# Six writes of x to DRAM, issued by ScalarE instead of SyncE

## The chip, the core and the metric

The kernel runs on one core of a Trainium2 chip. The time is that of one execution on the device in microseconds (us); the median of three runs before the change is 434.64 us (432.01 to 434.95). The trace is of one further execution of its own.

## What is computed

Three layers follow each other, all in float32: an attention with a decaying state (8 heads), a feed-forward layer with a short convolution as its gate, and a mixture of eight experts in which each token goes to one expert. The last two, cut to what matters here:

```python
def _moe_ref(x, w_in, conv_w, w_out):            # feed-forward with a gate
    h = np.maximum(x @ w_in, 0.0)
    ...
    gate = 1.0 / (1.0 + np.exp(-conv_out))       # conv over 3 neighbours in the sequence
    return (h * gate @ w_out)                    # the x of the next layer

def _moe2_ref(x, w_gate, w_local, w1, w2):       # one of 8 experts for each token
    ...
    for s in range(S):
        ...                                      # e: the token's expert, or the previous one's
        h = np.maximum(x[b, s] @ w1[e], 0.0)
        out[b, s] = p[e] * (h @ w2[e])
```

There are 2 batches of 768 tokens, 512 features, and 1024 hidden features in either layer.

## The kernel before

Attention and the feed-forward layer keep their data on the chip. The feed-forward output of a batch is made in six token tiles t = 0 to 5 of 128 tokens each (`ffn_out`): 24 matmuls add up a tile of 128 x 512 in PSUM (`x2_ps`, x_ps in the profile), ScalarE copies it to a tile in SBUF, and a DMA writes it to xs, a buffer in DRAM, whose rows are in the order of tokens. For t = 4 and 5 of the second batch (b = 1) the SBUF tile is one of two that stay (xl4, xl5, kept in `LAST`); for all others it is one of two buffers named xn, so that the third copy waits until the first write has landed.

While the second batch is in `ffn_out`, VectorE works out which expert each token has (`route`, then `tables`): ScalarE's two copies kp feed a scan on VectorE, a chain of small VectorE operations and four small groups of matmuls on TensorE follow, and at the end stand `ei` (the expert of each tile of tokens, read by SyncE to address weights) and `it` (the token numbers of each tile, read by GpSimd's gathers).

The expert stage then works on 11 tiles of 128 gathered tokens and two groups of four quarter tiles. GpSimd gathers a tile's rows from xs (`gather`, tile xg); the first two gathers read only rows of the tokens up to t = 3 of the second batch, and what belongs to t = 4 and 5 is added from xl4 and xl5 by matmuls (`begin_x`, `late_x`). Those first two start the stage on TensorE (L813). All later gathers read all of xs, so they wait for all six writes.

The weights of an expert are loaded by SyncE into a few buffers: `fetch(j, which)` issues four loads of 512 KB into a tile r, one for each (tile j modulo 2, which of the two matrices); `fetch_q` issues four such loads into a quarter buffer, qc or qs1l by turns. From the third tile on, a `fetch` carries a condition: where the same lane already holds that expert, its four loads are issued and move nothing. ScalarE and VectorE cut r into a high and a low part (`cut`, L717 and L718, tiles ws0h, ws0l, ws1h, wc), and TensorE multiplies with both.

The order on each engine is that of the code. SyncE therefore issues, in this order: the r loads of `fetch(0, 0)` and `fetch(0, 1)` (L698), the writes of t = 0, 1 and 2 of the second batch (L491), the loads of `fetch(1, 0)` (their address needs `ei`), the write of t = 3, four quarter loads qc (L708), the writes of t = 4 and 5, then `fetch(1, 1)`, four loads qs1l, and so on. A DMA issue waits on its engine's queue for its data, and everything behind it waits too. Each DMA also takes the next of eight counting semaphores by turns (DMAHW0 to DMAHW7 below) and waits until the DMA that had the same one eight DMAs earlier has landed.

Of the kernel before, what the change touches and what calls it, by code (L numbers as in the profile page):

```python
# [19 lines left out]
B, H, S, D = 2, 8, 768, 64  # L20
# [3 lines left out]
P = 128  # L24
# [67 lines left out]
def tile_kernel(ctx, tc, cat, cst, qT, kT, kN, vN, w_in, conv_w, w_out, wg, w1, w2, out):  # L92
    nc = tc.nc
    te, ve, se, po, sy = nc.tensor, nc.vector, nc.scalar, nc.gpsimd, nc.sync
# [11 lines left out]
    xs = dram.tile([NT, DM], F32, name="xs")  # L106
# [24 lines left out]
    def mm3(ps, lhi, llo, rhi, rlo, first, last):  # L131

        te.matmul(ps, lhi, rhi, start=first, stop=False)  # L133
        te.matmul(ps, lhi, rlo, start=False, stop=False)  # L134
        te.matmul(ps, llo, rhi, start=False, stop=last)  # L135
# [338 lines left out]
    def ffn_out(b, t, ms):  # L474

        ts = slice(t * P, (t + 1) * P)
        if ms[0] == 0:
            OUT[b, t] = psb.tile([P, DM], F32, tag="x2", name="x2_ps")
        ps = OUT[b, t]
        for m in ms:  # L480
            g = hg[b, m]
            mm3(ps, g[:, 0, ts], g[:, 1, ts], wo_hi[:, m, :], wo_lo[:, m, :], m == 0, m == 7)
        if ms[-1] == 7:
            if b == B - 1 and t >= NG - 2:
                xn = xpool[0].tile([P, DM], F32, name=f"xl{t}", bufs=1)
                LAST.append(xn)
            else:
                xn = rt.tile([P, DM], F32, name="xn", bufs=2)
            se.activation(out=xn, in_=OUT.pop((b, t)), func=AF.Copy)  # L489
            r = b * S + t * P  # L490
            sy.dma_start(out=xs[r:r + P, :], in_=xn)  # L491

    one_p = rt.tile([P, 12, P], F32R, name="one_p")
    mr = rt.tile([RK + E, S], F32R, name="mr")
# [248 lines left out]
    for t in range(2):  # L743
        ffn_out(0, t, range(6))
# [3 lines left out]
    for n, (t, ms) in enumerate(units, 1):  # L748
        ffn_out(0, t, ms)
        if n % 2 == 0 and n < 14:  # L750
            tick()
        if n in (3, 5, 7):
            next(side, done)
# [5 lines left out]
    for t in range(2):  # L759
        ffn_out(1, t, range(4))  # L760
# [302 lines left out]
```

## Time and profile before

| | before |
|---|---|
| median of three runs | 434.64 us (432.01 to 434.95) |
| the profiled execution | 432.95 us, of which the span of the trace is 431.2 us |
| TensorE (PE) busy | 408.8 us, 95% of the span |
| VectorE (DVE) busy | 289.6 us, 67% |
| ScalarE (ACT) busy | 259.2 us, 60% |
| GpSimd (POOL) busy | 91.5 us, 21% |
| moved by DMA | 86.59 MB, 201 GB/s over the span |
| granted clock of TensorE | 0.99 of full speed |

Times in rows count from the start of the span. In a timeline, each row has the start, the duration, the engine, the line of the program, the operation, the tile written and the tiles read, how many instructions are merged into the row, and in brackets how long the engine was idle before it and what released it. SPq is SyncE's queue of DMA issues. The feed-forward layer of the second batch ends at 244, and the expert stage fills the rest.

### The profile page before, as it was taken

To read this page: it belongs to the slowest core of one execution; us is meant where nothing else is said; L and a number is where in the kernel's file an instruction comes from. 1 tells how busy PE (TensorE), PEld (TensorE's weight loads), DVE (VectorE), ACT (ScalarE), POOL (GpSimd) and SP (SyncE) were. 2 spreads that over 40 slices of the span, in tenths; PEclk is the share of its full clock that TensorE was granted. 3 is DMA by queue.
4 is the path that set the end of the run, shared out by engine and by line. 5 is a ranking of instruction groups with operands and counts; after the bars stand their busy time and mean duration, and the time that the engine had idled before them with its cause. 6 is when DMAs were issued, how large, how long until landed. Compare 5 with 4: busy or idle time off the path is not lost.

```text
span 431.2 us, 7291 instructions
## 1 busy us (share of the span) xinstructions
PE 408.8 (95%) x2412; PEld 329.2 (76%) x2412; DVE 289.6 (67%) x518; ACT 259.2 (60%) x429; POOL 91.5 (21%) x92
## 2 busy tenths in 40 slices
PE   8898999999899999999999999999999999999991
PEld 7787897899798778988768776867738677776880
DVE  3798789787767260377899058968664796858650
ACT  2787677667666212566704166869556686958560
POOL 5256664211110000000000330305203132211210
PEclk9999999999899999999999999999999999999997
DMA  7989763230000101000197899999969999774100
GB/s 229 388 291 398 260 211 92 93 97 1 2 0 2 49 26 49 26 0 2 58 377 254 304 373 379 342 390 409 398 254 340 407 364 346 280 260 186 44 25 29
DMA packets 27324, 86.59 MB, mean 201 GB/s; under 512 B 3598, under 2 KB 4622, under 8 KB 27280
## 3 DMA queue, kind: packets, MB, share of 16 engines
q1 hardware_dynamic: 25200, 79.76, 50.4%
q0 software_dynamic: 2080, 6.29, 3.9%
q8 instruction: 21, 0.34, 0.3%
q14 instruction: 23, 0.19, 0.1%
HBM read 105.18 MB, written 6.55 MB: 259 GB/s over the span
## 4 chain that ended last, share of the span: by engine, by line
PE 35%; issue 26%; DMA 15%; DVE 14%; ACT 4%; POOL 3%; SPq 1%; POOLq 0%; DVEq 0%; ACTq 0%
DMA out_dram<-yo,it 13%; PE h_ps L133 5%; PE h_ps L134 4%; PE h_ps L135 4%; PE x_ps L133 4%; PE x_ps L134 3%; PE x_ps L135 3%; PE y L300 3%; DVE cc L353 3%; PE s_ps L282 2%; POOL xg L727 2%; PE inc L290 1%; DMA kq<-in_qT_dram 1%; PE y L302 1%; DVE na L149 1%
## 5 line engine op out<-in xcount | busy, mean ns | idle before, releaser
L133 PE MATMUL h_ps<-xT,wih 128*128 128x384 f32 x128 | 46.9, 366 | 0.0
L353 DVE SCALAR_TENSOR_TENSOR cc<-h,cw,cc 128x768 f32<-128x768 f32 x32 | 34.4, 1075 | 18.6 <-ACT cc L350 18.5
L863 POOL DMA_INDIRECT out_dram<-yo,it x13 | 16.7, 1282 | 136.3 <-ACT yo L862 136.3
L727 POOL DMA_INDIRECT xg<-xs,it x13 | 18.8, 1444 | 123.4 <-DMA qc<-in_w_dram 115.8
L134 PE MATMUL h_ps<-xT,wih 128*128 128x384 f32 x128 | 43.5, 340 | 0.0
L135 PE MATMUL h_ps<-xT,wil 128*128 128x384 f32 x128 | 43.4, 339 | 0.0
L133 PE MATMUL x_ps<-woh,hg 128*128 128x512 f32 x96 | 38.5, 401 | 0.0
L134 PE MATMUL x_ps<-wol,hg 128*128 128x512 f32 x96 | 37.6, 391 | 0.0
L135 PE MATMUL x_ps<-woh,hg 128*128 128x512 f32 x96 | 37.5, 391 | 0.0
L718 DVE TENSOR_TENSOR ws0l<-r,ws0l 128x1024 fp32r<-128x1024 f32 x22 | 26.0, 1221 | 16.3 <-ACT ws0l L717 16.2
L153 POOL TENSOR_TENSOR na<-na,raw 128x512 int32<-128x512 int32 (+1 forms) x17 | 21.9, 1289 | 48.9 <-ACT raw L151 17.7
L300 PE MATMUL y<-at,vz 128*128 128x128 f32 x192 | 30.6, 281 | 1.8 <-ACT vz L277 0.9
L718 DVE TENSOR_TENSOR ws0h<-r,ws0h 128x1024 fp32r<-128x1024 f32 x22 | 26.0, 1221 | 8.2 <-ACT ws0h L717 8.2
L718 DVE TENSOR_TENSOR wc<-r,wc 128x1024 fp32r<-128x1024 f32 x22 | 25.9, 1221 | 8.0 <-ACT wc L717 8.0
L717 ACT ACTIVATE ws0l<-r 128x1024 fp32r<-128x1024 f32 x22 | 22.1, 1052 | 13.9 <-PE y L135 13.9
L282 PE MATMUL s_ps<-qz,kq 128*128 128x256 f32 x96 | 29.2, 386 | 1.0 <-issue 1.0
L718 DVE TENSOR_TENSOR ws1h<-r,ws1h 128x1024 fp32r<-128x1024 f32 x22 | 26.0, 1221 | 6.0 <-ACT ws1h L717 3.8
L717 ACT ACTIVATE wc<-r 128x1024 fp32r<-128x1024 f32 x22 | 22.1, 1054 | 11.3 <-PE g L135 11.3
L300 PEld LDWEIGHTS y<-at,vz 128*128 128x128 f32 x192 | 25.4, 191 | 4.3 <-DVE xT L305 2.3
L284 DVE TENSOR_TENSOR at<-s_ps,ca 128x256 f32<-128x256 f32 x48 | 20.2, 420 | 11.7 <-PE s_ps L282 11.6
L133 PEld LDWEIGHTS h_ps<-xT,wih 128*128 128x128 f32 x128 | 24.6, 192 | 3.1 <-issue 1.8
L489 ACT ACTIVATE xn<-x_ps 128x512 f32<-128x512 f32 x10 | 6.0, 599 | 32.8 <-PE x_ps L135 18.2
(231 smaller groups left out, 1044.9 us busy)
## 6 DMA issues: line engine op xcount, KB each, us to landing
r<-in_w_dram SPq DMA_DIRECT2D x88, 512.0 KB
qc<-in_w_dram SPq DMA_DIRECT2D x32, 512.0 KB
qs1l<-in_w_dram SPq DMA_DIRECT2D x32, 512.0 KB
raw<-in_w_in_dram SPq DMA_DIRECT2D x8, 512.0 KB
raw<-in_w_out_dram SPq DMA_DIRECT2D x8, 512.0 KB
kq<-in_qT_dram SPq DMA_DIRECT2D x7, 384.0 KB
kq<-in_kT_dram SPq DMA_DIRECT2D x7, 384.0 KB
kv<-in_vN_dram SPq DMA_DIRECT2D x7, 384.0 KB
```

The lines of the kernel that those rows point to most:

```text
L133: te.matmul(ps, lhi, rhi, start=first, stop=False)
L134: te.matmul(ps, lhi, rlo, start=False, stop=False)
L135: te.matmul(ps, llo, rhi, start=False, stop=last)
L153: po.tensor_tensor(out=a, in0=a, in1=lo, op=ALU.add)
L282: te.matmul(ps, self.kq[:, 0, tok], self.qz[:, :, tok], start=True, stop=True)
L284: ve.tensor_tensor(out=self.at[c], in0=ps, in1=self.dm, op=ALU.mult)
L300: te.matmul(y, vz[:, c, j, :], at[:, j, :], start=(j == 0), stop=(c == 0 and j == 1))
L353: ve.scalar_tensor_tensor(out=cc, in0=h[:, i:i + S], scalar=cw[:, m, i:i + 1], in1=cc, op0=ALU.mult, op1=ALU.add)
L717: se.activation(out=w[:, 0, h, :], in_=r, func=AF.Copy)
L718: ve.tensor_tensor(out=w[:, 1, h, :], in0=r, in1=w[:, 0, h, :].bitcast(F32), op=ALU.subtract)
L727: return po.indirect_dma_start(out=xg, out_offset=None, in_=xs[0:n], in_offset=bass.IndirectOffsetOnAxis(ap=it[:, j:j + 1], axis=0), bound ...
L863: po.indirect_dma_start(out=out, out_offset=bass.IndirectOffsetOnAxis(ap=it[:, j:j + 1], axis=0), in_=yo, in_offset=None, bounds_check=NT ...
```

## The change

The write of x is issued by ScalarE (`se`) where the batch is the last one, and by SyncE (`sy`) elsewhere:

```diff
             se.activation(out=xn, in_=OUT.pop((b, t)), func=AF.Copy)
             r = b * S + t * P
-            sy.dma_start(out=xs[r:r + P, :], in_=xn)
+            (se if b == B - 1 else sy).dma_start(out=xs[r:r + P, :], in_=xn)
```

On ScalarE, from the softmax's exponential of the second batch (ex) onwards. xn is the tile copied from PSUM, kp the two copies that VectorE's scan reads:

```order
 L527 ACTIVATE ex<-d 128x48
 L489 ACTIVATE xn<-x_ps 128x512
+L491 DMA xs<-xn 128x512
 L535 ACTIVATE kp<-sp_2175 8x384
 L535 ACTIVATE kp<-sp_2176 8x384
-L489 ACTIVATE xn<-x_ps 128x512 x2
+L489 ACTIVATE xn<-x_ps 128x512
+L491 DMA xs<-xn 128x512
+L489 ACTIVATE xn<-x_ps 128x512
+L491 DMA xs<-xn 128x512
 L717 ACTIVATE ws0h<-r_2117 128x1024 x2
 L489 ACTIVATE xn<-x_ps 128x512
```

Each write stands right behind its copy; that of t = 0 now stands ahead of both kp.

On SyncE, between the quarter loads qc and the address of the loads r that follow them (TENSOR_LOAD ei reads an expert's number, ISA rows work out the address):

```order
 L708 ISA
 L708 DMA qc_2404<-in_w_dram 128x1024
-L491 DMA xs<-xl_2478 128x512
-L491 DMA xs<-xl_2506 128x512
 L679 TENSOR_LOAD ei
 L679 ISA x2
```

The two writes of t = 4 and 5 are gone from between the loads, and so are, further up, those of t = 0 to 3.

The first load of r behind them, in the program after the change, with what it waits for (semaphores of DMAs and of engines):

```order
L708 DMA qc_2404<-in_w_dram 128x1024 [waits DMAHW5_49]
L679 TENSOR_LOAD ei
L679 ISA x2
L698 ISA
L698 DMA r_2539<-in_w_dram 128x1024 [waits DMAHW6_49,PE_49]
```

The load now follows the qc loads directly and waits for TensorE, which reads what stood in the place of its buffer.

## Rows read from the trace of the kernel before

**Rows 1.** The page, busy time of TensorE in us, share, instructions

```profile
PE 408.8 (95%) x2412; PEld 329.2 (76%) x2412; DVE 289.6 (67%) x518; ACT 259.2 (60%) x429; POOL 91.5 (21%) x92
```

**Rows 2.** Timeline of SyncE's queue, 226 to 262

```profile
228.74 1.95 SPq L698 DMA_DIRECT2D r<-in_w_dram  x4
232.45 0.34 SPq L491 DMA_DIRECT2D xs<-xn  x1
233.58 4.00 SPq L708 DMA_DIRECT2D qc<-in_w_dram  x4
239.24 5.78 SPq L491 DMA_DIRECT2D xs<-xl  x2
245.85 2.97 SPq L698 DMA_DIRECT2D r<-in_w_dram  x4
```

**Rows 3.** Busy time in stretches; last two columns DMA's busy share, GB/s

```profile
224.00:230.00 6.00, 5.18 (x24) 3.95 (x23) 5.55 (x28) 2.50 (x3) 0.00 (x0) 1.00 0.55 204
...
244.40:247.50 3.10, 2.68 (x24) 2.71 (x25) 0.00 (x0) 0.27 (x1) 0.04 (x1) 1.00 0.47 120
...
262.00:310.00 48.00, 48.00 (x280) 33.90 (x273) 36.27 (x36) 35.89 (x47) 10.30 (x9) 1.00 0.99 385
...
319.00:324.00 5.00, 4.75 (x18) 1.35 (x19) 0.89 (x1) 0.67 (x1) 0.00 (x0) 1.00 0.20 56
```

**Rows 4.** Timeline of GpSimd, the first gather

```profile
239.27 1.21 POOL L727 DMA_INDIRECT xg<-xs,it  x1 [115.81 <-DMA qc<-in_w_dram]
```

**Rows 5.** Chain of work that ended last: start, us, what

```profile
244.69 2.00 DMA xs<-xl
...
247.47 1.00 POOL xg L727
```

**Rows 6.** Timeline of TensorE, its waits between 224 and 246

```profile
225.64 0.40 PE L621 MATMUL pb<-tb,cs 8*128 8x64 f32 x2 [0.82 <-DVE pi L558]
244.82 1.13 PE L813 MATMUL tp<-cs,xg 128*128 128x128 f32 x8 [0.79 <-DMA xg<-xs,it]
```

**Rows 7.** Timeline of ScalarE, 213 to 245

```profile
213.82 0.60 ACT L489 ACTIVATE xn<-x_ps 128x512 f32<-128x512 f32 x1 [0.45 <-PE x_ps L135]
214.68 0.85 ACT L535 ACTIVATE kp<-sp 8x384 f32<-8x384 f32 x2 [0.26 <-PE sp L532]
...
226.69 0.60 ACT L489 ACTIVATE xn<-x_ps 128x512 f32<-128x512 f32 x1 [8.07 <-DMA xs<-xn]
...
232.32 2.00 ACT L717 ACTIVATE ws0l<-r 128x1024 fp32r<-128x1024 f32 x2
...
244.07 0.60 ACT L489 ACTIVATE xl<-x_ps 128x512 f32<-128x512 f32 x1 [4.85 <-PE x_ps L135]
```

**Rows 8.** Timelines of TensorE and of SyncE's queue, 255 to 291

```profile
261.21 1.93 PE L892 MATMUL hq_ps<-qc,xq 128*32 128x512 f32 x16
...
263.19 3.69 SPq L708 DMA_DIRECT2D qc<-in_w_dram  x4
267.73 4.16 SPq L708 DMA_DIRECT2D qs1l<-in_w_dram  x4
...
286.54 3.68 SPq L708 DMA_DIRECT2D qs1l<-in_w_dram  x4
```

**Rows 9.** Timeline of TensorE, two quarter groups and what follows each

```profile
301.86 1.90 PE L914 MATMUL yq_ps<-qs1l,tq 128*32 128x512 f32 x16
303.69 0.50 PE L133 MATMUL y<-ws0l,th 128*128 128x512 f32 x1
...
317.90 3.24 PE L914 MATMUL yq_ps<-qs1l,tq 128*32 128x512 f32 x6
...
323.17 0.50 PE L133 MATMUL y<-ws0l,th 128*128 128x512 f32 x1
```

**Rows 10.** Chain of work that ended last, SyncE's first issues

```profile
1.19 0.42 SPq L234
1.66 0.42 SPq L236
```

**Rows 11.** Timeline of VectorE, the scan and the cut ws0l

```profile
215.19 0.94 DVE L540 TENSOR_TENSOR_SCAN mr<-kp,sp 8x384 fp32r<-8x384 f32 x1 [0.95 <-PE sp L532]
...
235.78 2.35 DVE L718 TENSOR_TENSOR ws0l<-r,ws0l 128x1024 fp32r<-128x1024 f32 x2
```

**Rows 12.** Line 698, 226 to 262: duration in ns, least, median, most

```profile
L698 SPq DMA_DIRECT2D r<-in_w_dram x16: 73/333/1357, 228.7 to 262.0; - x16
```

**Rows 13.** Tile xg, its gathers between 225 and 262

```profile
DMA to landing us min/median/max: 4.0/6.5/8.1
```

## The prediction

> **What bounds the kernel now.** I read the page first: TensorE is busy for 408.8 of 431.2 us [rows 1]. A TensorE that is busy for 95% of the span leaves little for a transfer to win, so the question is where TensorE stands still because of these six writes, directly or through what they delay. I therefore went from the writes outwards: the two queues that issue DMAs (SyncE and GpSimd), ScalarE, which makes the data, and TensorE, which waits for the gathers that read it.
>
> SyncE issues everything in program order. From 232.45 it carries, one behind the other, the write of token tile t = 3, four quarter-tile loads, the writes of t = 4 and 5, and then the loads r of the next stage [rows 2]. The row at 239.24 with 5.78 us holds both writes xl: SyncE issues that of t = 4 and then stands until ScalarE has copied t = 5, and only then can it go on to the r loads at 245.85. In those 5.8 us nothing new is loaded, and the DMA engines are 0.47 busy in 244.4 to 247.5 [rows 3]. That is the first thing the change can win.
>
> The second is on the way to TensorE. The first gather starts at 239.27 on GpSimd [rows 4]. It needs the writes of t = 0 to 3 in DRAM, and that of t = 3 was issued at 232.45: 6.8 us from issue to the reader's start. The row names a load of qc as releaser; that load is not among what the gather reads, the write ahead of it on the same queue is. On an empty queue a write takes 2.00 us from issue to landing, and the reader starts 0.78 us behind that (244.69 + 2.00 = 246.69; start at 247.47) [rows 5]. So some 4 us of the 6.8 are waiting behind loads. TensorE waits for this gather: 0.79 us of idle time ahead of 244.82 [rows 6].
>
> The third wait looks larger and is worth nothing: ScalarE stood idle for 8.07 us ahead of its copy of t = 2 at 226.69, released by the write of t = 0 (two buffers xn) [rows 7]. TensorE never waited for that copy: its wait in this stretch is 0.82 us at 225.64, and that is for VectorE's routing chain [rows 6].
>
> **The change, part by part.** *Six issues leave SyncE.* That chain of r loads no longer stands behind the copy of t = 5. What then holds it is its buffer, on top of tiles that TensorE reads in the matmuls of t = 5; so it goes out somewhere between 239.24 and 244.69, where it went out at 245.85: 1.2 to 6.6 us earlier. The qc loads at 233.58 no longer wait for the copy of t = 3; those of r at 228.74 can go when the expert numbers are read. DMA had a lull there too (0.55 busy in 224 to 230) [rows 3].
>
> *Where that lead goes.* I follow it along SyncE. The next load that needs something of TensorE is qc at 263.19: its buffer is read by the sixteen matmuls that start at 261.21 and last 1.93 us, to 263.14 [rows 8]. The load left 0.05 us later. However far SyncE has run ahead, it stands here until TensorE is through; from here it is ahead by what TensorE is ahead, no more. One thing may still be kept: the four qs1l issues at 267.73 took 4.16 us, the same four at 286.54 took 3.68 [rows 8]. I take the 0.48 us as one issue held by a full queue, and with fewer bytes outstanding I expect it to go.
>
> *What a lead is worth later.* There is one place in the expert stage where TensorE waits long for loads. The matmuls on qs1l of a quarter group take 303.69 - 301.86 = 1.83 us when their weights are there; those that start at 317.90 take 323.17 - 317.90 = 5.27 us [rows 9]. The loads are 3.44 us late. DMA is 0.99 busy in 262 to 310 and 0.20 in 319 to 324 [rows 3]. If the loads come earlier by G and 0.48 us and TensorE by G, the wait shrinks by 0.48 us.
>
> *Six issues come to ScalarE.* An issue at the start of SyncE's program takes 0.47 us from one to the next (1.19, 1.66) [rows 10]. Five of the six cost nothing: behind the copies of t = 1, 4 and 5 ScalarE idles, and the issue behind that of t = 3 pushes the cut ws0l, done at 232.32 + 2.00 = 234.32, to 234.8, where VectorE takes it up at 235.78 [rows 7, 11]; the cut behind t = 2 has more room still. If that cover were gone, each would cost its 0.47 us. The first is on the path. It stands between the copy of t = 0, which ends at 213.82 + 0.60 = 214.42, and the two copies kp that start at 214.68 [rows 7]; VectorE's scan waits for them at 215.19 [rows 11], and the routing chain from there is what TensorE waits for at 225.64. With 0.02 us to react and 0.47 us to issue, kp starts at 214.91: 0.23 us late, and TensorE is 0.23 us late from 225.64 on. If an issue on ScalarE costs as much as the longest load issue of the stage, 1.36 us [rows 12], it is 1.1 us. That is the upper bound; the lower one is nothing. I take 0.23, since a write's issue on SyncE is short (0.34 us at 232.45).
>
> *When the write of t = 3 lands.* Issued by ScalarE at about 232.5, it is no longer behind the r loads in one queue, but beside them. No row shows a write from ScalarE. Bounds: 2.00 us on an idle queue, and 2.00 + 4.1 = 6.1 where loads press, since the gathers, which have their own queue too, land after 4.0 to 8.1 us [rows 13], a spread of 4.1. That is 234.5 to 238.6, and the gather starts 0.78 later, at 235.3 to 239.4. I take the middle, 237.3. The gather itself then takes 4.0 to 8.1 us; with the 5.5 us that lie between 239.27 and the first matmul behind it at 244.82, that matmul could start at 242.8, before ScalarE's copy at 244.07 shows TensorE through with t = 5 [rows 7]. So the 0.79 us go.
>
> The Trainium skill ("DMA: Bandwidth & Descriptors", section "Queues, rings and completion order") says that SyncE and ScalarE each have a row of rings and that a DMA engine goes round between rows packet by packet. By it the write would be served in turn with the loads and would land, as an estimate, 0.6 us behind the idle-queue time; the spread of the gathers in rows 13 speaks for a slower share.
>
> *Sum.* TensorE ahead by 0.79 - 0.23 = 0.56 us, and 0.48 us of the later wait: 1.04 us. The profiled execution took 432.95 us (span 431.2), so 431.9 by its own count; it lies 1.7 us below the median of the runs shown, 434.64, which gives **433.6 us**. About 1% (4.3 us) is what a measurement here can tell from no change, and this is a quarter of it.
>
> **The rivals.** *The lead survives.* If qc at 263.19 is not held, or SyncE's lead is kept in DMA that is always full, the whole 3.44 us goes: 434.64 - 0.56 - 3.44 = 430.6. For it: DMA is 0.99 busy from 262 to 310 [rows 3], so what is ahead there has no gap to lose its lead in. Against it: the 0.05 us between TensorE's end and the issue.
>
> *Nothing moves.* The write lands as late as before because the loads take the engines anyway, 0.79 is not won, and only 0.23 is lost and at most 0.48 gained: 434.4 to 434.9. For it: the upper bound of the landing, 238.6, is where it was. The Trainium skill (same page, "Issuing engines are not separate DMA queues") would say this of the change: DMAs of all issuing engines share the engines and interleave, so that spreading them saves only the sequencer's time; the row at 239.24 shows that what is saved here is a wait on the sequencer, which such a rule does not price.
>
> *The other side: the gather comes later than now.* The qc and r loads now run ahead, DMA is full up to 244, and the write or the gather gets a small share. With both at their upper bounds the gather starts at 239.4 and lands at 247.5, 2.7 us behind 244.82: 434.64 + 0.23 + 2.7 - 0.48 = 437.1. If the write is served only once the loads have drained at about 244, it is some 439. It decides from a landing of the gather after 244.8; each microsecond beyond costs one. Against it: in rows 13 the second queue was always served beside full loads.
>
> *ScalarE's issue is dear.* At 1.36 us in front of kp, with 0.48 kept: 434.64 - 0.79 + 1.1 - 0.48 = 434.5, and with nothing won elsewhere 435.7.
>
> **How the numbers follow.** Main course 0.50; the lead survives 0.10; nothing moves 0.24; gather later 0.10; dear issue 0.06. The predicted time is the first's, 433.6. The range goes down to the second, 430.6, and up to the dear issue with nothing won and the lesser part of the late gather, 436.4; what is outside is the rest of the late gather and the runs' own spread (432.0 to 434.95). Over 1% faster (under 430.3) needs the surviving lead and a lucky run: 0.05. Over 1% slower (over 439) needs the late gather at its worst: 0.06. The rest is within 1%.
>
> **What the profile of the changed kernel would show.** SyncE's r loads leave before 245; if they do not, the wait on the buffer was the binding one. The first gather starts at 236 to 238, and the idle time ahead of the first matmul on xg is under 0.1 us. kp starts about 0.2 us behind its former place relative to the copy ahead of it. DMA is busy through 244 to 247. The qc issue still stands within 0.1 us of the end of the matmuls that free its buffer. The late quarter group takes about 4.8 us instead of 5.27. I am wrong in kind if that group takes 1.8 us (the lead was kept) or if the matmuls on xg start after 245.

## The result and the profile after

The changed kernel is slower: 438.53 us (median of 10 runs, 435.39 to 440.66) against 434.55 (432.01 to 435.81), a ratio of 1.0088 with a 95% interval of 1.0060 to 1.0117. Ratios, here and below, leave out executions in a disturbed state of the device, so they need not be the quotient of the medians. The difference is under the 1% that the prediction took as the least that can be told from no change; the interval is clear of 1 all the same. The prediction was 433.6, with a range up to 436.4. The profiled execution took 438.02 us, of which the span is 436.3.

The page, TensorE's busy time:

```profile
PE 411.0 (94%) x2412; PEld 332.1 (76%) x2412; DVE 289.5 (66%) x518; ACT 259.6 (60%) x429; POOL 92.4 (21%) x92
```

TensorE has the same 2412 matmuls as before [rows 1]. It is busy 2.2 us longer with them (411.0 against 408.8) and stands still 25.3 us of the span instead of 22.4. To find where, I measure from one event that both traces have, ScalarE's copy of token tile t = 5, to the first matmul g of the expert stage. That also takes out what differs ahead of it: the copy starts at 244.07 in the trace before [rows 7] and at 245.67 here, of which 0.15 us is the change (the copies of t = 0 and 5 lie 30.25 us apart before, 30.40 after) and the rest lies earlier and differs from execution to execution. First the kernel before (TensorE, then GpSimd's second gather):

```profile
246.68 1.06 PE L813 MATMUL tp<-cs,xg 128*128 128x128 f32 x8
...
250.21 0.50 PE L133 MATMUL g<-ws0h,xh 128*128 128x512 f32 x1
```

```profile
241.31 1.01 POOL L727 DMA_INDIRECT xg<-xs,it  x1 [0.28 <-POOL xg L726]
```

Then the kernel after (timelines of TensorE and of ScalarE; ACTq is ScalarE's queue of DMA issues):

```profile
227.25 0.40 PE L621 MATMUL pb<-tb,cs 8*128 8x64 f32 x2 [0.88 <-DVE pi L558]
248.23 2.05 PE L813 MATMUL tp<-cs,xg 128*128 128x128 f32 x8 [2.60 <-DMA xg<-xs,it]
250.07 1.71 PE L819 MATMUL tp<-oh,xl 128*128 128x128 f32 x8
252.01 1.13 PE L813 MATMUL tp<-cs,xg 128*128 128x128 f32 x8 [0.22 <-DMA xg<-xs,it]
252.98 2.84 PE L819 MATMUL tp<-oh,xl 128*128 128x128 f32 x24
255.61 0.49 PE L133 MATMUL g<-ws0h,xh 128*128 128x512 f32 x1
```

```profile
215.27 0.60 ACT L489 ACTIVATE xn<-x_ps 128x512 f32<-128x512 f32 x1 [0.45 <-PE x_ps L135]
215.90 0.35 ACTq L491 DMA_DIRECT2D xs<-xn  x1
216.29 0.85 ACT L535 ACTIVATE kp<-sp 8x384 f32<-8x384 f32 x2 [0.43 <-PE sp L532]
234.01 0.33 ACTq L491 DMA_DIRECT2D xs<-xn  x1
245.67 0.60 ACT L489 ACTIVATE xl<-x_ps 128x512 f32<-128x512 f32 x1 [4.85 <-PE x_ps L135]
```

From the copy of t = 5 to g: 6.14 us before (250.21 - 244.07), 9.94 after (255.61 - 245.67). That is +3.80 us, as much as the medians differ (3.98). From g to the end of the span nothing is lost: 180.99 before, 180.69 after. The 3.80 have two parts. Up to the first matmul on the gathered tile it is +1.81 (2.56 against 0.75: the wait for the first gather is 2.60 us instead of the 0.79 of [rows 6]). From there to g it is +1.99 (7.38 against 5.39): the first sixteen matmuls take 2.05 and 1.71 us, where [rows 6] has 1.13 for the first eight, and then the second gather is waited for (0.22 us). So it is the second gather that sets g here: its reader starts 6.34 us behind the copy, 2.61 before, and that +3.73 is nearly the whole. The matmuls that took longer ahead of it cost nothing in this trace, since the second gather lands at 251.9 (244.16 + 7.7) whatever they take.

The queues show why. GpSimd's gathers, SyncE's queue, and the stretches in the windows (DMA's busy share and GB/s are the last two columns, the column before them TensorE's granted clock):

```profile
242.12 1.21 POOL L727 DMA_INDIRECT xg<-xs,it  x1 [117.79 <-DMA qc<-in_w_dram]
244.16 1.01 POOL L727 DMA_INDIRECT xg<-xs,it  x1 [0.28 <-POOL xg L726]
```

```profile
232.29 3.73 SPq L708 DMA_DIRECT2D qc<-in_w_dram  x4
242.93 2.12 SPq L698 DMA_DIRECT2D r<-in_w_dram  x4
245.91 3.72 SPq L708 DMA_DIRECT2D qs1l<-in_w_dram  x4
```

```profile
244.40:247.50 3.10, 1.24 (x6) 0.68 (x4) 0.00 (x0) 0.60 (x1) 1.31 (x2) 1.00 0.93 326
247.00:250.00 3.00, 1.77 (x8) 1.80 (x9) 0.00 (x0) 0.00 (x0) 0.00 (x0) 0.67 1.03 384
250.00:253.00 3.00, 2.78 (x19) 2.62 (x18) 0.00 (x0) 0.00 (x0) 0.00 (x0) 0.76 1.03 413
```

Before, the r loads left 1.78 us behind the copy of t = 5 (245.85 [rows 2], 244.07). Now they leave 2.74 us ahead of it, at 242.93, between the two gathers. Before, DMA was 0.98 busy from 239.3 to 244.4. Then came the lull of [rows 3], 0.47 busy from 244.4 to 247.5, and at its start the two gathers landed (5.4 and 4.0 us behind their issue). It is 0.93 busy now: the loads are in it. The second gather is issued at 244.16 and its reader starts at 252.01; the two land 6.0 and 7.7 us behind their issue.

A second trace of the same kernel (439.12 us, span 437.3) shows the two parts larger:

```profile
247.87 1.13 PE L813 MATMUL tp<-cs,xg 128*128 128x128 f32 x8 [3.71 <-DMA xg<-xs,it]
248.83 1.49 PE L819 MATMUL tp<-oh,xl 128*128 128x128 f32 x8
250.98 2.05 PE L813 MATMUL tp<-cs,xg 128*128 128x128 f32 x8 [0.65 <-DMA xg<-xs,it]
252.82 4.42 PE L819 MATMUL tp<-oh,xl 128*128 128x128 f32 x24
257.03 0.50 PE L133 MATMUL g<-ws0h,xh 128*128 128x512 f32 x1
```

```profile
250.00:253.00 3.00, 2.35 (x11) 2.08 (x11) 0.00 (x0) 0.00 (x0) 0.53 (x1) 0.50 1.03 420
253.00:256.00 3.00, 3.00 (x16) 3.00 (x15) 0.00 (x0) 0.00 (x0) 2.57 (x4) 0.50 1.03 419
```

The copy of t = 5 starts at 244.19 here, so copy to g is 12.84 us, and from the copy to the end of the span it is 193.11 (187.13 before, 190.63 in the first trace). The last matmuls ahead of g run at half the clock (1.2 GHz, 0.50 in both rows): 2.05 and 4.42 us where the first trace has 1.13 and 2.84 for the same matmuls. That is 2.5 us in which no gather is waited for, so here the half clock is paid in full.

### The profile page after: what moved, and what is told of

Read it like the earlier page. It is cut to its first block, busy times and chain, and to the rows that moved or that the text cites. A ratio compares the mean times of both kernels' runs of the same rounds, so it can differ in the third digit from the quotient of the medians.

```text
span 436.3 us, 7289 instructions
## 1 busy us (share of the span) xinstructions
PE 411.0 (94%) x2412; PEld 332.1 (76%) x2412; DVE 289.5 (66%) x518; ACT 259.6 (60%) x429; POOL 92.4 (21%) x92
## 4 chain that ended last, share of the span: by engine, by line
PE 34%; issue 27%; DMA 16%; DVE 14%; ACT 4%; POOL 2%; SPq 1%; POOLq 0%; DVEq 0%; ACTq 0%
DMA out_dram<-yo,it 14%; PE h_ps L133 5%; PE h_ps L134 4%; PE h_ps L135 4%; PE x_ps L133 4%; PE x_ps L135 3%; PE x_ps L134 3%; PE y L300 3%; PE s_ps L282 2%; DVE cc L353 2%; DVE na L149 2%; DMA kq<-in_qT_dram 1%; PE inc L290 1%; DVE na L150 1%; PE y L302 1%
## 5 line engine op out<-in xcount | busy, mean ns | idle before, releaser
L300 PEld LDWEIGHTS y<-at,vz 128*128 128x128 f32 x192 | 25.3, 191 | 4.3 <-DVE xT L305 2.4
```

The lines of the kernel that those rows point to most:

```text
L300: te.matmul(y, vz[:, c, j, :], at[:, j, :], start=(j == 0), stop=(c == 0 and j == 1))
```

## The experiments

The theory was: SyncE's standing at its writes held the loads behind them back; without it they run ahead onto the two gathers that TensorE waits for. The first rival: writing from ScalarE is itself slow or costs time on the path. The last column is the stretch from the copy of t = 5 to g in the trace of one execution (two of the change, four of e8); each ratio is against the kernel before, run beside it. The traces of e2 and e4 are of short executions (431.53 and 431.82 us). Inserted lines shift the line numbers in some kernels by up to 6 (L816 and L819 are then the L813 of the kernel before).

| kernel | median, us (runs) | before, us | ratio, 95% interval | copy to g, us |
|---|---|---|---|---|
| before | | | | 6.14 |
| the change | 438.53 (10) | 434.55 | 1.0088 (1.0060 to 1.0117) | 9.94, 12.84 |
| e1_hold_all | 435.27 (12) | 434.25 | 1.0014 (0.9990 to 1.0038) | 6.06 |
| e2_hold_t5 | 434.24 (12) | 434.25 | 1.0000 (0.9975 to 1.0025) | 5.62 |
| e3_act_45 | 436.46 (12) | 434.25 | 1.0039 (1.0004 to 1.0074) | 9.47 |
| e4_act_03 | 433.76 (12) | 434.25 | 0.9990 (0.9965 to 1.0015) | 5.37 |
| e7_act_04 | 434.00 (12) | 434.42 | 1.0006 (0.9983 to 1.0029) | 5.42 |
| e8_r_first | 437.52 (6) | 434.42 | 1.0095 (1.0058 to 1.0132) | 7.58, 6.67, 11.94, 11.78 |
| e9_hold_half | 437.01 (6) | 434.42 | 1.0086 (1.0053 to 1.0119) | 7.86 |
| e5_r_behind_t3 | 436.19 (12) | 434.42 | 1.0045 (1.0017 to 1.0074) | 5.11 |
| e12_filler | 437.35 (6) | 433.87 | 1.0087 (1.0061 to 1.0113) | 10.27 |
| e15_filler3 | 436.78 (11) | 434.33 | 1.0066 (1.0030 to 1.0102) | 11.94 |

**Give SyncE its waits back (e1, e2).** Behind each write that ScalarE issues, SyncE issues a DMA of 256 bytes from the same tile to a spare buffer fz: in e2 for t = 5 alone, in e1 for all six (`range(6)` in place of `(5,)`).

```diff
             (se if b == B - 1 else sy).dma_start(out=xs[r:r + P, :], in_=xn)
+            if b == B - 1 and t in (5,):
+                sy.dma_start(out=fz[t:t + 1, :], in_=xn[0:1, 0:64])
```

> All six writes are issued by ScalarE, as in the change, and SyncE gets at each write's old place a DMA of 256 bytes that reads the same tile: it holds SyncE back as the write did and moves next to nothing. If the loss comes from SyncE running ahead with its loads (theory), the gathers come as early as before and the ratio is 0.998 to 1.002. If ScalarE's own way of writing is slow or its issues cost time on the path (rival), the holds change nothing: 1.004 to 1.009.

> As the change, with one such DMA of 256 bytes on SyncE at the place of the write of t = 5 only: the r loads behind it are held until ScalarE has copied t = 5, the qc loads are not. Theory: the two gathers have the quiet DMA again and land as fast as before, and what is left of the loss is the later start of the first gather, 1.25 us or up to 1.9 us: ratio 1.002 to 1.005. Rival (a slow way of writing or of issuing on ScalarE): no better than the change, 1.008.

e1 came out as the theory had it (1.0014). e2 did better than it: 1.0000, where 1.002 to 1.005 was expected. TensorE's first matmul on the gathered tile in e1, then in e2:

```profile
247.84 1.13 PE L816 MATMUL tp<-cs,xg 128*128 128x128 f32 x8 [0.71 <-DMA xg<-xs,it]
```

```profile
243.77 1.13 PE L816 MATMUL tp<-cs,xg 128*128 128x128 f32 x8
```

e1 has the wait of the kernel before (0.71 against 0.79 us), e2 has none. One wait of SyncE, that for the copy of t = 5, is all that separates e2 from the change, so it is the absence of this wait that brings the loss. The qc loads run ahead in e2 too, and that alone does no harm: the gather starts later (3.64 us ahead of the copy of t = 5, 4.80 before), but lands 3.5 us behind its issue, and the wait of 0.79 us is gone.

**Split the six writes (e3, e4, e7).** ScalarE issues only t = 4 and 5 in e3, t = 0 to 3 in e4 (`t < NG - 2`), t = 0 to 4 in e7 (`t < NG - 1`).

```diff
-            (se if b == B - 1 else sy).dma_start(out=xs[r:r + P, :], in_=xn)
+            (se if b == B - 1 and t >= NG - 2 else sy).dma_start(out=xs[r:r + P, :], in_=xn)
```

> Only the writes of t = 4 and 5 go to ScalarE; those of t = 0 to 3 stay on SyncE. The first two gathers read nothing that these two writes make. Theory: the r loads run ahead into the lull in which the two gathers landed, the gathers land later, and TensorE waits some 2 to 3 us more: ratio 1.004 to 1.007. Rival (slow writes on ScalarE): the gathers' own data come as before, 1.000 within 0.002.

> Only the writes of t = 0 to 3 go to ScalarE; those of t = 4 and 5 stay on SyncE and hold the r loads as before. Theory: the first gather starts up to 1.25 us later, since the qc loads run ahead of the write of t = 3, and the gathers themselves are as fast as before: ratio 1.001 to 1.004. Rival (slow writes or dear issues on ScalarE): these four carry the loss, 1.006 to 1.009.

> The writes of t = 0 to 4 go to ScalarE, that of t = 5 stays on SyncE, where it holds the r loads until ScalarE has copied t = 5. Theory (the r loads that run ahead of the copy of t = 5 are the whole loss, and the qc loads that run ahead are a small gain): ratio 0.997 to 1.001, and no idle time of TensorE ahead of its first matmul on xg. Rival (the six writes each carry a part of the loss): 1.005 to 1.008, five sixths of it.

In e3 the first two gathers read nothing that ScalarE writes, and TensorE waits for both; in e4 four of the six writes have moved, and nothing is late. e3, then e4 (TensorE, GpSimd's first gather and the lull):

```profile
248.87 1.13 PE L813 MATMUL tp<-cs,xg 128*128 128x128 f32 x8 [3.10 <-DMA xg<-xs,it]
...
251.67 1.13 PE L813 MATMUL tp<-cs,xg 128*128 128x128 f32 x8 [0.78 <-DMA xg<-xs,it]
```

```profile
239.61 1.21 POOL L727 DMA_INDIRECT xg<-xs,it  x1 [116.82 <-DMA qc<-in_w_dram]
```

```profile
243.36 1.13 PE L813 MATMUL tp<-cs,xg 128*128 128x128 f32 x8
```

```profile
244.00:247.00 3.00, 3.00 (x28) 2.94 (x27) 0.00 (x0) 0.11 (x1) 0.09 (x1) 1.00 0.61 175
```

e3 has both waits and 9.47 us from copy to g. Its median is below that of the change, with intervals that overlap, and its ratio is at the lower edge of what was expected; its trace ran at full clock. Part of the 9.47 us may not be the edit's: the first gather starts 3.58 us ahead of the copy of t = 5 instead of 4.80, on a path that e3 leaves alone (e8 below has executions of both kinds). In e4 the first gather takes at most 3.75 us from its issue to its reader (243.36 - 239.61), where before it was 5.55 (239.27 to 244.82), and TensorE waits for nothing. e4 expected a later gather and a loss of 0.4 to 1.7 us: the gather does start later, 3.90 us ahead of the copy of t = 5 instead of 4.80, and nothing is lost. e7 adds t = 4, and again nothing is lost. So five of the six writes can move without harm; the loss comes only when the sixth moves too.

**The loss without ScalarE (e8).** All writes stay on SyncE; `ffn_out` leaves the write of t = 5 in a list HELD5, and it is issued behind the r loads.

```diff
         fetch(1, 1)
+        HELD5.pop()()
         fetch_q(0, 0, 1)
```

> All writes stay on SyncE, as in the kernel before; only the order of its code changes: the write of t = 5 moves behind the four r loads that followed it, so that these leave some 2.9 us earlier, as they do after the change. ScalarE issues nothing. Theory: the loss is there without ScalarE, ratio 1.003 to 1.009, and TensorE waits 2 to 4 us ahead of its first matmul on xg. Rival (the loss belongs to the queue of ScalarE): 1.000 within 0.002.

> A second trace of the kernel with all writes on SyncE and the write of t = 5 behind the r loads. Its first trace was of its fastest execution (434.81 us, median 437.5) and shows only 0.5 us more between ScalarE's copy of t = 5 and the end of the span than before (187.63 against 187.13). Theory: an ordinary execution shows 189 to 191, with the loss ahead of the matmuls on xg. If it shows 187 to 188 again, the loss of the median lies ahead of the copy, and the theory does not explain this run.

> A third trace of the kernel with the write of t = 5 behind the r loads. Its two traced executions took 434.8 and 435.2 us and waited 2.0 and 1.1 us for the first two gathers at full clock; the four that were only timed took 435.6 to 439.8. If the rest of the loss is TensorE's clock, an execution of over 437 us shows a granted clock of 0.5 between 245 and 256 and one of under 436 shows 1.00.

> A fourth trace of the same kernel, for the same question: over 437 us with the granted clock at 0.5 between 245 and 256, under 436 us with 1.00.

1.0095: the loss is there with ScalarE issuing nothing. Its size differs between executions. The two that were traced first took 434.81 and 435.21 us, with waits of 0.4 to 1.3 us for each of the two gathers and the clock at 1.00. From the copy of t = 5 to the end of the span they have 187.63 and 188.19 us; e10 expected 189 to 191, and missed. This is the first:

```profile
246.02 1.13 PE L819 MATMUL tp<-cs,xg 128*128 128x128 f32 x8 [0.69 <-DMA xg<-xs,it]
...
249.35 1.13 PE L819 MATMUL tp<-cs,xg 128*128 128x128 f32 x8 [1.31 <-DMA xg<-xs,it]
```

The third and fourth took 440.50 and 439.30 us, with waits of 3.94 and 3.91 us and half the clock behind them, as expected of executions of over 437. The third:

```profile
249.30 2.05 PE L819 MATMUL tp<-cs,xg 128*128 128x128 f32 x8 [3.94 <-DMA xg<-xs,it]
```

```profile
250.00:253.00 3.00, 3.00 (x16) 3.00 (x15) 0.00 (x0) 0.00 (x0) 0.00 (x0) 0.50 1.03 407
```

From the copy to the end the third has 193.31 us, the fourth 192.34. The copy of t = 5 and the r loads come at the same time in the first and the third (copies at 245.37 and 245.39). The gathers do not. GpSimd's gathers and SyncE's r loads, in the first and then in the third:

```profile
240.46 1.21 POOL L733 DMA_INDIRECT xg<-xs,it  x1 [115.65 <-DMA qc<-in_w_dram]
242.63 1.92 SPq L704 DMA_DIRECT2D r<-in_w_dram  x4
```

```profile
242.31 1.21 POOL L733 DMA_INDIRECT xg<-xs,it  x1 [118.18 <-DMA qc<-in_w_dram]
242.65 1.93 SPq L704 DMA_DIRECT2D r<-in_w_dram  x4
244.34 1.01 POOL L733 DMA_INDIRECT xg<-xs,it  x1 [0.28 <-POOL xg L732]
```

In the first both gathers (the second at 242.50) start ahead of the loads; in the third the loads leave between the two, as in the change. All traces in which all four r loads leave ahead of the copy or all behind it, those with added matmuls and e5 left out, fall into four groups by this:

| r loads leave | first gather starts ahead of the copy of t = 5 by | copy to g, us |
|---|---|---|
| behind the copy (before, e1) | 4.7 to 4.8 us | 6.1 |
| behind the copy (e2, e4, e7) | 3.6 to 3.9 us | 5.4 to 5.6 |
| 2.7 us ahead of it (e8, first two) | 4.9 to 5.0 us | 6.7, 7.6 |
| 2.7 us ahead of it (the change, e3, e8's other two) | 3.1 to 3.6 us | 9.5 to 12.8 |

So a later gather alone costs nothing, the loads ahead of the copy with an early gather cost 0.5 to 1.4 us, and the two together 3.3 to 6.7. These are copy-to-g times of single executions, and within e8 the two kinds were seen, not made by an edit. In e8 the two kinds part well ahead of the gather: the copy of t = 2 waits 8.13 and 8.25 us for the write of t = 0 to land in the first two, 9.62 and 9.71 in the others, and the r loads of the first lane leave 1.4 to 1.5 us later behind it. Why that write lands later in some executions stays open.

**Half of the loads (e9).** As e2, with the DMA of 256 bytes between the second and the third of the four r loads.

```diff
         for i in range(4):
+            if (j, which, i) == (1, 1, 2):
+                sy.dma_start(out=fz[0:1, :], in_=LAST[1][0:1, 0:64])
             sy.dma_start(out=dst[:, i, :], in_=src[:, i * 1024:(i + 1) * 1024], **kw)
```

> As the change, with a DMA of 256 bytes on SyncE that reads the tile of t = 5, between the second and the third of the four r loads: two of them run ahead, two are held. If what counts is how many bytes of loads are under way beside the two gathers, the loss is about half of that with none held: 1 to 2.5 us, ratio 1.002 to 1.006. If any load ahead of the gathers makes them late by the full amount, 1.008; if two loads fit in the lull, 1.000.

```profile
246.88 1.13 PE L816 MATMUL tp<-cs,xg 128*128 128x128 f32 x8 [1.40 <-DMA xg<-xs,it]
...
249.78 1.13 PE L816 MATMUL tp<-cs,xg 128*128 128x128 f32 x8 [0.88 <-DMA xg<-xs,it]
```

The trace has about half of the loss (7.86 us, +1.72), the times have all of it (1.0086; the traced run, 436.06, is the shortest of the six). Whether the loss goes with the bytes stays open; that two loads of 512 KB are enough for a loss is shown.

**Let the gather start earlier (e5).** All writes on SyncE; the r loads of the first lane move behind the write of t = 3.

```diff
-        if n == 8:
+        if n == 12:
             fetch(1, 0)
```

> All writes on SyncE as before; the four r loads of the first lane (those that stood just ahead of the write of t = 3) are moved behind that write, so that it lands with little ahead of it. By the prediction's reading the first gather then starts some 3 to 4 us earlier and the 0.79 us of idle time of TensorE go: ratio 0.998. If the gather's own time under loads is what counts and not its start, the loads that now follow later lie on the gathers, and it is 1.000 to 1.004.

GpSimd's first gather, and the matmuls on a later gathered tile:

```profile
236.84 1.21 POOL L727 DMA_INDIRECT xg<-xs,it  x1 [112.65 <-DVE pr L665]
```

```profile
259.75 0.66 PE L800 MATMUL tp<-cs,xg 128*128 128x128 f32 x4 [3.37 <-DMA xg<-xs,it]
```

The gather no longer waits for a write (the row names VectorE, whose tables give the token numbers), and the wait of 0.79 us is gone, as the prediction's reading of an earlier gather had it. But the r loads now go out at 235.07 instead of 228.74, just ahead of the qc loads, and the writes of t = 4 and 5 land behind all eight. The third gather starts at 252.82 instead of 247.47, and TensorE waits 3.37 us for a later tile: 1.0045, the second of the two expectations and a little more. The trace is of one of the shorter of twelve executions (434.48 us) and has only 0.30 us more than before from the copy of t = 5 to the end of its span (187.43), so it does not show the whole of that loss.

**The half clock (e12, e15).** The change, with matmuls whose result nobody reads ahead of the first matmul on xg: six in e12, three in e15.

```diff
+        busy = psq.tile([P, 2, 512], F32, tag="q", name="busy")
+        for k in range(6):
+            te.matmul(busy[:, 0, :], ident, LAST[0], start=True, stop=True, skip_group_check=True)
         for j in range(2):
             begin_x(j)
```

> The changed kernel with six matmuls of TensorE added whose result nobody reads; they stand ahead of the first matmul on xg and need only xl4, so they run in the 2.6 to 3.7 us in which TensorE waits for the first gather. Both traces of the changed kernel show TensorE's granted clock at half (0.50) for 3.4 and 6.4 us right behind that wait. If the half clock adds to the loss (theory now): the clock stays at 1.00 there, the added matmuls are free, and the ratio falls from 1.0088 to 1.003 to 1.007. If the loss is the wait alone: 1.008 to 1.010, no better than the change.

> The changed kernel with three of the added matmuls instead of six. Six took 5.31 us, 2 us more than the wait, so that what they kept in clock they cost in time; three take 2.65 us and fit into the wait of 2.6 to 3.7 us. If the half clock adds to the loss: the granted clock stays at 1.00 from 244 to 256, the stretch from ScalarE's copy of t = 5 to the first matmul g takes 8 to 9 us (9.9 and 12.8 in the two traces of the change, 6.1 before), and the ratio is 1.004 to 1.007. If the wait alone counts: 1.008 to 1.010.

e12, then e15:

```profile
244.77 5.31 PE L940 MATMUL busy<-xl,cs 128*128 128x512 f32 x12
249.92 1.05 PE L813 MATMUL tp<-cs,xg 128*128 128x128 f32 x8
```

```profile
243.52 2.74 PE L940 MATMUL busy<-xl,cs 128*128 128x512 f32 x6
246.55 1.13 PE L813 MATMUL tp<-cs,xg 128*128 128x128 f32 x8 [0.30 <-DMA xg<-xs,it]
...
250.47 1.13 PE L813 MATMUL tp<-cs,xg 128*128 128x128 f32 x8 [1.89 <-DMA xg<-xs,it]
251.43 4.47 PE L819 MATMUL tp<-oh,xl 128*128 128x128 f32 x24
```

With six, the clock stays at full and the matmuls from 249.92 to g take 5.32 us, as before the change (5.39), but the six take 5.31 us, longer than either wait of the change (2.60 and 3.71), and the time is no better: 1.0087, on the side of "the wait alone". With three, the first wait is filled, but the second gather is waited for, and the clock halves behind that wait instead (4.47 us against 2.84); copy to g is 11.94 us where 8 to 9 was expected. 1.0066, with an interval that holds the full loss as well as a third of it. So neither run separates the two. The traces show that the half clock follows the waiting and adds to it in some executions (2.5 us in the second trace of the change, nothing in the first). How much of the median is its doing was not settled.

No version beat the kernel before by more than can be measured; e4, at 0.9990, is the nearest.

## Why the prediction was wrong

What happened is the rival "the gather comes later than now", priced at 437.1 to 439 and given 0.10, and the sign that the prediction gave for being wrong in kind: the matmuls on xg start after 245, at 248.23. That the price holds the measured 438.53 is in part luck: it has the first gather 2.7 us late, which is 1.81 us late in the first trace, and neither the second gather nor the clock. By the prediction's own steps:

- **The six issues on ScalarE: right.** An issue takes 0.33 to 0.35 us, and kp starts 1.02 us behind the copy's start instead of 0.86, 0.16 us later (0.23 predicted). TensorE's wait at pb is 0.88 (0.82 before).
- **The wait of 8.07 us ahead of the copy of t = 2: worth nothing, right.** It is gone, and the matmuls behind come no earlier.
- **The r loads leave earlier: right.** They leave 4.5 us earlier against the copy of t = 5, inside the 1.2 to 6.6.
- **The lead is lost at the next qc load: right.** The matmuls that free its buffer, and the load on SyncE's queue:

```profile
266.62 1.92 PE L892 MATMUL hq_ps<-qc,xq 128*32 128x512 f32 x16
```

```profile
268.61 3.70 SPq L708 DMA_DIRECT2D qc<-in_w_dram  x4
```

  It leaves 0.07 us behind their end (268.54). So the loads that ran ahead onto the gathers bought nothing later, and the rival in which the lead survives is out.
- **The late quarter group, 4.8 us: wrong, by little.** From 323.31 to the matmul that follows it at 328.48 it takes 5.17 us, 5.27 before; 0.10 of the 0.48 us.

```profile
323.31 1.25 PE L914 MATMUL yq_ps<-qs1l,tq 128*32 128x512 f32 x4
...
328.48 0.50 PE L133 MATMUL y<-ws0l,th 128*128 128x512 f32 x1
```

- **The write of t = 3: too small a term.** I took the middle of two bounds, a gather that starts 4.8 us behind the issue. It starts 8.1 us behind it (234.01 to 242.12), beyond my upper bound of 6.9. The lower bound, 2.00 us "on an empty queue", was not read on an idle one either: it is from the lull, where DMA was 0.47 busy. The Trainium skill ("DMA: Bandwidth & Descriptors", section "Queues, rings and completion order") has the two queues served in turn, by which I worked out a landing of 2.6 us as an estimate, a gather some 3.4 us behind the issue; the 8.1 us do not show that. This term also left out that the qc loads now leave ahead of this write (232.29, 234.01) and no longer behind it. In e1, where they wait again, ScalarE's write is 6.99 us ahead of its gather (235.51, 242.50), as SyncE's was (6.82). By itself this error costs nothing: in e4 the gather starts 7.8 us behind the issue (231.84, 239.61), and TensorE does not wait. But it puts the r loads between the two gathers, and e8 shows that to be the dear case.
- **The gather's own 5.5 us: here the sum failed.** I took the time between the gather's start and its reader from the trace before, 239.27 to 244.82, and added it to the new start. In that trace the loads had just drained when it landed (DMA is 0.98 busy from 239.3 to 244.4 and 0.24 from there to 245.85), and nothing followed them: SyncE stood at the write of t = 5. The change takes away that very wait. I counted the lull as waste ("nothing new is loaded") and forecast that DMA would be busy through it, without asking who was using it: the two gathers, which land there. With the r loads in it, the first is 6.1 us from its start to its reader (242.12 to 248.23), the second 7.9 (244.16 to 252.01). The second has 5.4 before (241.31 to 246.68), with no wait. I followed only the first gather, and it is the second that sets g. Of the 3.73 us by which its reader is later, 1.25 are the later start of the gathers (3.55 us ahead of the copy of t = 5 instead of 4.80) and 2.48 the longer way of the second.
- **The term that nothing in the trace before showed** is the half clock behind the longer wait: 2.5 us in the second trace, nothing in the first.

What was right was hidden by this: with the write of t = 5 left on SyncE (e4, e7), copy to g is 5.37 and 5.42 us, 0.72 to 0.77 us less than before, which is the 0.79 us that the prediction hoped for. The times do not show it: 0.9990 and 1.0006, with intervals that hold both.

## What to carry to other kernels

A queue that stands at a wait also holds back what is behind it, and that can be what keeps the DMA engines free for a transfer that the bounding engine waits for. Before taking such a wait away, list what will leave earlier, where it will be in flight, and which transfers land in that stretch now; a duration read where a transfer lands in a lull does not hold once the change fills the lull. And ask what the lead buys: here the loads had to stand for a buffer 25 us later, so coming early won nothing.

## What the runs showed of the hardware

A write of 256 KB from ScalarE's own queue was 7.8 to 8.5 us from its issue to the start of the gather that reads it in the eight traces where SyncE's qc loads had left ahead of it, and 7.0 us in e1, where they left behind it. SyncE's own write behind the r loads took 6.7 to 6.8 (before, e8, e10) or 8.0 to 8.5 us (e3, e13, e14); in the lull, with DMA 0.47 busy, a write and the start of its reader were 2.78 us apart. A queue of its own did not bring the write past the loads.

A gather of 128 rows landed 3.5 to 3.6 us behind its issue in e2, e4 and e7 (DMA 0.62 busy in e4, from 239.6 to 243.4), and 6.0 to 7.7 us behind it in the change, with the r loads beside it (DMA 0.93 to 1.03 busy).

TensorE's granted clock fell to half behind waits of 2.6 to 3.9 us on this path (the two traces of the change, the third and fourth of e8) and behind waits of 0.30 and 1.89 us in e15, and stayed at 1.00 in e3 with waits of 3.10 and 0.78 us. So a longer wait for DMA can cost twice, and the second part differs from execution to execution.
